# A mixture-of-experts item whose token columns are gathered by GpSimd instead of by transposes and matmuls on TensorE

## The chip, the core and the metric

The program runs on one core of a Trainium2 chip. The metric is the device time of one execution in microseconds (us). Two executions of the same kernel differ by a few tenths of a per cent. TensorE is called PE in the rows, VectorE DVE, ScalarE ACT, GpSimd POOL and SyncE SP; PEld is PE's weight load, and a q behind an engine's name is that engine's sequencer, which loads registers, branches and issues work.

## What is computed

```python
attn = sigmoid(q @ k.T / 8 - log(448)) @ v        # 4 batches, 12 heads, 448 tokens, 64 per head
x = attn as [1792 tokens, 768]
# first layer: tokens with x @ w_skip > 0 go to expert argmax(x @ w_gate)
x[sel] += gate * (relu(x[sel] @ w1[e]) @ w2[e])   # w1[e] 768 x 1024, w2[e] 1024 x 768
# second layer: expert by cosine similarity; its result is the output
out = gate * (relu(x @ v1[e]) @ v2[e])
```

In each layer every token has one of 8 experts. With these inputs, the first layer works on batches 2 and 3 alone: all 448 tokens of batch 2 share an expert, and of batch 3 there are 407 tokens of one expert and 41 of another. In the second layer three batches are of one expert each, and batch 2 has 443 tokens of one and 5 of another.

## The kernel before

Activations lie transposed: `xT` is [128, 6, 1792], with 768 = 6 x 128 features on the partitions and one column for each token. After the attention there are **blocks**, one for a batch and its most frequent expert: block 0 and block 1 of the first layer, then four blocks of the second. `dense` runs a block over eight slices `f` of 128 hidden features. `h(f)` is 18 matmuls (each product is three, since both factors are split in a rounded part and the rest, `mm3`), `y(f-1)` is 18 more that accumulate in six PSUM banks `YS`. Between them stand **sub-steps** 0 to 15: `sub(2f)` behind `h(f)` and `sub(2f+1)` behind `y(f-1)`. Sub-steps 0 and 1 both stand behind `h(0)`, since there is no `y` yet. What is handed to a sub-step is written into every engine's program at that place. The order is written by hand: `schedule` takes a dictionary of steps by sub-step (`at`) and a list of further steps (`prep`) with the sub-steps they go to. Each engine runs its own list in order.

The tokens of a batch that are not of the block's expert are an **item** of up to 64 tokens (`Item`). Item 0 (the 41 tokens) is run beside block 1, item 1 (the 5 tokens) beside the last block. An item needs its tokens as 64 columns `XB` of 6 x 128 features. Before, this is made so:

- `regs` loads batch, expert and position from the list `LI` in SBUF into registers of DVE, ACT and SP. `copy` copies the batch's columns from `xT` to the tile `STG` (three copies on DVE, three on ACT).
- `select` makes on DVE the 0/1 matrices `SEL`, which say which of 4 x 112 tokens goes to which of 64 places, and `GRC`, which holds each token's gate and its row number less 4096.
- Six `turn`s transpose `STG` on PE into token rows `ROW`, with one ACT copy each. `gather` (16 matmuls by `SEL`) picks the 64 rows, `gatherT` (3 transposes) turns them back into columns in a part of `ROW`.
- `gate` makes the gates and, for item 0, the transposed `SEL`.
- `first` and `second` load the expert's two weight matrices in four quarters. `h(0)`, `h(1)` (24 matmuls each) compute two halves of the hidden features, `hT` transposes them (2 transposes and a DVE copy), and behind the block `finish` runs the 32 matmuls of the second product, `y`.

In the profiled lines, item 0 has `regs` and `copy` at sub-step 3, `turn` at 4 to 9, `select` at 7, `gather` at 10, `gatherT` and `gate` at 11, `h(0)` at 12, `hT(0)` at 13, `h(1)` at 14, `hT(1)` at 15. Item 1 has `regs` and `copy` at 1, `turn` at 2 to 7, `select` at 5, `gather` at 8, `gatherT` at 9, `gate` at 10, the rest as item 0. Behind block 1 stands `add_y`, six DVE additions of `YS` to `xT`, and then the item's `y`, which writes `YS[0]`. Behind the last block stand copies of `YS` to `STG` (ACT and DVE in turn), transposes, scaled rows in `ROW`, two stores (one of SP, one of ACT), then the item's `y` and its scattered store, which waits for both.

Two PSUM banks (`bank`) serve `h(f)` and all small steps in turn: whoever takes a bank waits for those who read it last.

Of the kernel before, what the change touches and what calls it, by code (L numbers as in the profile page):

```python
# [12 lines left out]
I32 = mybir.dt.int32  # L13
AF = mybir.ActivationFunctionType
ALU = mybir.AluOpType
# [6 lines left out]
def sigmoid_attention_moe_moe_kernel(  # L22
# [15 lines left out]
    nc = tc.nc  # L38
# [26 lines left out]
    def bank(name):  # L65
        if not BANKS:
            return psA.tile([128, 512], F32, tag="psA", name=name)
        turn[0] ^= 1
        return BANKS[turn[0]]

    def spare():
        turn[1] ^= 1
        return XG[turn[1]]
# [428 lines left out]
    def merge(*steps):  # L502

        out = {}
        for t in steps:
            for k in sorted(t):
                f = t[k]
                out.setdefault(k, []).extend(f if isinstance(f, list) else [f])
        return out

    def schedule(at, prep, slots):

        assert len(slots) == len(prep)
        return merge(at, *({k: f} for k, f in zip(slots, prep)))
# [166 lines left out]
    def batch_cols(p, b):  # L681
        return xT[:, p, :].rearrange("q (b s) -> q b s", s=S)[:, ds(b, 1), :].rearrange("q o s -> q (o s)")
# [74 lines left out]
    ROW = wp.tile([128, C * DM], F32, tag="row", name="row")  # L757
    SELT = wp.tile([128, S], F32R, tag="selT", name="selT")
    SEL = wp.tile([128, 4 * 128], F32, tag="sel", name="sel")
    XB = ROW[:, 3 * DM : 3 * DM + ND * TL].rearrange("p (c t) -> p c t", t=TL)  # L760
    SMALL = wp.tile([128, 16], F32, tag="small", name="small")
    POSC, GS, IDX = SMALL[:P, 0:C], SMALL[:, 12:14], SMALL[:, 14:15].bitcast(I32)
    GRC = SMALL[:P, 4:12].rearrange("p (c t) -> p c t", t=2)
# [105 lines left out]
    class Item:  # L869


        def __init__(self, m, i):
            self.m, self.i = m, i
            self.wa, self.wb, self.R = (w1, w2, R1) if m == 0 else (v1, v2, R2)

        def regs(self):
            L, i, xe = self.R.LI, self.i, [ENG.Activation, ENG.DVE]
# [18 lines left out]
                    self.wb[ds(self.e, 1), u * 256 : (u + 1) * 256, :].rearrange("o (g p) d -> p (o g) d", p=128),  # L896
                )

        def copy(self):
            for d in range(ND):  # L900
                o = STG[:, d * S : (d + 1) * S]
                if d % 2:
                    nc.vector.tensor_copy(o, batch_cols(d, self.b))
                else:
                    nc.scalar.activation(o, batch_cols(d, self.b), AF.Copy)

        def select(self):
            R, j = self.R, self.j
            nc.vector.tensor_single_scalar(
# [15 lines left out]
                self.R.LI[0:1, ds(self.i + NL, 1)], engines=[ENG.DVE], min_val=0, max_val=NE - 1  # L925
            )

        def turn(self, d):


            def f():
                ps = bank("ps_xn")
                for c in range(C):
                    o = d * S + c * P
                    nc.tensor.transpose(ps[:P, c * 128 : (c + 1) * 128], STG[:, o : o + P], ident)
                o = ROW[:P].rearrange("p (c d) -> p c d", c=C)[:, :, d * 128 : (d + 1) * 128]
                nc.scalar.activation(o, ps[:P, :].rearrange("p (c d) -> p c d", c=C), AF.Copy)

            return f

        def gather(self):

            hw = DM // 2
            ps = bank("ps_xg")
            for c in range(C):
                for g in range(2):
                    nc.tensor.matmul(
                        ps[TL * g : TL * g + TL, :hw], lhsT=SEL[:P, c * 128 : c * 128 + TL],
                        rhs=ROW[:P, c * DM + g * hw : c * DM + g * hw + hw], start=c == 0, stop=c == C - 1,
                    )  # L950
            self.xg = spare()
            nc.scalar.activation(self.xg[:, :hw], ps[:, :hw], AF.Copy)

        def gatherT(self):
            ps = bank("ps_xs")
            for i in range(3):
                nc.tensor.transpose(ps[:, i * 128 : i * 128 + 128], self.xg[:, i * 128 : i * 128 + 128], ident)
            nc.scalar.activation(
                XB.rearrange("p (g i) t -> p i g t", g=2), ps[:, :384].rearrange("p (i g t) -> p i g t", i=3, g=2), AF.Copy
            )  # L960

        def gate(self):
            ps = bank("ps_gs")
# [10 lines left out]
        def h(self, s):  # L974


            def f():
                ps = bank("ps_h2")
                for c in range(ND):
                    for g in range(2):  # L980
                        nc.tensor.matmul(
                            ps[TL * g : TL * g + TL, :256], lhsT=XB[:, c, :],
                            rhs=as1(QUART[2 * s + g])[:, c, :], start=c == 0, stop=c == ND - 1,
                        )
                hs = self.hs = spare()
                nc.scalar.activation(hs[:, :256], ps[:, :256], AF.Relu)

            return f
# [37 lines left out]

        def ready(self, k0):

            prep = [self.turn(d) for d in range(ND)] + [self.gather, self.gatherT, self.gate]
            at = merge({k0: [self.regs, self.copy], k0 + 4: self.select}, {5: [lambda: self.first(0)]}, {  # L1030
                7: [lambda: self.first(1)], 9: [lambda: self.first(2)], 11: [lambda: self.first(3)],
                12: [self.h(0)], 13: [self.hT(0), lambda: self.second(0, 1)],
                14: [self.h(1)], 15: [self.hT(1), lambda: self.second(2, 3)],
            })
            return at, prep

        def now(self, hooks=()):

            hooks = list(hooks) + [None] * 3
            self.regs()  # L1040
            self.first(0, 1, 2, 3)
            self.copy()
            self.select()
            for f in self.ready(0)[1]:
                f()
            self.h(0)()
            self.hT(0)()
            self.second(0, 1)
            self.h(1)()
            self.hT(1)()  # L1050
            self.second(2, 3)
            self.finish(hooks)

        def finish(self, hooks):
# [97 lines left out]
    def units1(e):  # L1152
        def f(k):
            u, r = k // 4, k % 4
            if r == 0 and u + 2 < NU:
                load_unit(w1, w2, e, u + 2)
            if u + 1 < NU and r % 2 == 0:
                for g in split_unit(u + 1)[:3] if r == 0 else split_unit(u + 1)[3:]:
                    g()

        return f

    def beside(units, steps):
        steps = merge(steps)

        def sub(k):
            for i in (k - 0.5, k):
                if i == k:
                    units(k)
                for f in steps.get(i, ()):  # L1170
                    f()

        return sub
# [42 lines left out]
    def block1(j):  # L1216

        b, e = rest_regs(j - 1)
        xs = XST[j % 2]

        def r2():
            if j > 1:
                return {}
            f = route2_steps(0, XST[0])
            return at_subs((1, 4, 6, 2, 3, 5, 6, 8), f[:3] + f[6:])

        def general():
            with tc.If(count(R1) > 0) as cmp:
                it = Item(0, 0)
                at, prep = it.ready(3)  # L1230
                dense(xs, beside(units1(e), schedule(merge(r2(), at), prep, (4, 5, 6, 7, 8, 9, 10, 11, 11))))
                add_y(b)
                it.finish(start2(j > 1))
            with cmp.Else():
                dense(xs, beside(units1(e), r2()))
                add_y(b)
                for f in start2(j > 1):
                    f()
                nothing()
            rare()  # L1240

        def last():
            with tc.If(nc.values_load(R1.LI[0:1, 3 * NL + 3 : 3 * NL + 4], min_val=0, max_val=NL) > 0) as cmp:
                it = Item(0, 0)
                at, prep = it.ready(3)
                one, two, three = start2(j > 1)
                steps = schedule(merge({12: one, 14: three}, r2(), at), prep, (4, 5, 6, 7, 8, 9, 10, 11, 11))
                dense(xs, beside(units1(e), steps))
                add_y(b)
                it.finish([two, None, None])  # L1250
            with cmp.Else():
                general()

        if j == B - 1:
            last()
            return
        with tc.If(NB["n"] > j) as cmp:
            dense(xs, beside(units1(e), merge(r2(), next_dense(j))))
            add_y(b)
            block1(j + 1)  # L1260
        with cmp.Else():
            last()
# [113 lines left out]
    for j in range(B):  # L1376
# [36 lines left out]
            continue  # L1413
        with tc.If(count(R2) > 0) as cmp:  # L1414
            it = Item(1, 0)
            at, prep = it.ready(1)
            dense(xs, beside(units2, schedule(merge(todo, at), prep, (2, 3, 4, 5, 6, 7, 8, 9, 10))))
            finish(j, b, True)()
            it.finish([None] * 3)
            info = mybir.DependencyInfo(mybir.DependencyClass.Sync, mybir.DependencyReason.DATA)  # L1420
            tc.add_manual_dep(it.put().ins, STORES[0].ins.name, info, reason="the rows it lands on")
# [40 lines left out]
```

## Time and profile before

| what | us |
|---|---|
| median of 3 runs (lowest, highest) | 590.76 (589.76, 591.95) |
| the profiled execution | 592.26 |
| its span (first to last instruction) | 590.5 |
| PE busy | 573.4 (97%) |
| DVE busy | 304.9 (52%) |
| ACT busy | 276.3 (47%) |
| POOL busy | 7.5 (1%) |

Block 1 with item 0 lies between 220 and 301 us, the last block with item 1 between 497 and 581 us. Matmuls are pipelined, so what a step costs PE is read from start to start in the order of time, not from busy time. The granted clock of PE is 9 tenths or more in every slice of the page behind the first.

### The profile page before, as it was taken

The numbers are of one execution on the slowest core, as the hardware profiler recorded it, in microseconds if no ns is written. First come the engines' busy times: TensorE is split into PE (matmuls) and PEld (weight loads), VectorE is DVE, ScalarE is ACT, GpSimd is POOL, SyncE is SP. The second block draws the span as 40 slices with busy tenths as digits, with TensorE's granted clock in tenths as the row PEclk, the third lists the DMA queues.
The fourth block names the chain that finished last, engine by engine and source line by source line (L and its number), as shares of the span: only waits on it lengthen the run. The fifth ranks groups of instructions, "written<-read, shape, count | busy, mean of one in ns | idle before, by whom it ended". The sixth has DMA issues, their size and how long they took to land. (4 is left out here: it accounts for less than half of the span.)

```text
span 590.5 us, 9926 instructions
## 1 busy us (share of the span) xinstructions
PE 573.4 (97%) x3720; PEld 437.7 (74%) x3720; DVE 304.9 (52%) x770; ACT 276.3 (47%) x451; POOL 7.5 (1%) x15
## 2 busy tenths in 40 slices
PE   7999999999999999999999999999999999999993
PEld 4453644534499988988868999979997999898881
DVE  2443444246857677661359663587357663542131
ACT  3766676667932364541146322932365322543020
POOL 2010000000000000000000000000000000000000
PEclk7999999999999999999999999999999999999998
DMA  9988698975341414235553060713226060742433
GB/s 150 136 126 123 96 134 108 130 102 174 129 157 60 157 41 165 68 108 185 192 199 126 2 213 1 237 71 125 89 84 226 0 215 0 245 156 67 161 108 100
DMA packets 139862, 73.31 MB, mean 124 GB/s; under 512 B 103858, under 2 KB 129798, under 8 KB 139792
## 3 DMA queue, kind: packets, MB, share of 16 engines
q1 hardware_dynamic: 116384, 65.94, 42.0%
q10 hardware_dynamic: 23216, 6.43, 6.4%
q8 instruction: 37, 0.61, 0.5%
q14 instruction: 33, 0.27, 0.1%
q0 software_dynamic: 192, 0.07, 0.1%
HBM read 66.90 MB, written 5.70 MB: 123 GB/s over the span
## 5 line engine op out<-in xcount | busy, mean ns | idle before, releaser
L787 PE MATMUL bank<-xs,h 128*128 128x448 f32 x288 | 107.6, 374 | 1.8 <-DVE hl L808 0.5
L807 ACT ACTIVATE hh<-bank 128x448 fp32r<-128x448 f32 x48 | 26.0, 542 | 176.4 <-PE bank L789 165.8
L787 PE MATMUL y<-hh,h 128*128 128x448 f32 x288 | 108.5, 377 | 0.0
L788 PE MATMUL y<-hl,h 128*128 128x448 f32 x288 | 105.6, 367 | 0.0
L789 PE MATMUL y<-hh,l 128*128 128x448 f32 x288 | 105.6, 367 | 0.0
L788 PE MATMUL bank<-xs,h 128*128 128x448 f32 x288 | 105.5, 366 | 0.0
L789 PE MATMUL bank<-xs,l 128*128 128x448 f32 x288 | 105.2, 365 | 0.1
L607 ACT ACTIVATE A<-psS,bias 128x896 f32<-128x896 f32 x84 | 83.5, 1007 | 36.3 <-PE psS L603 35.9
L603 PE MATMUL psS<-qT,kT 64*64 64x448 f32 x672 | 90.5, 554 | 0.0
L808 DVE SCALAR_TENSOR_TENSOR hl<-bank,hh 128x448 fp32r<-128x448 f32 x48 | 29.9, 623 | 113.5 <-ACT hh L807 111.9
L778 DVE TENSOR_TENSOR l<-r,h 128x512 fp32r<-128x512 f32 (+1 forms) x115 | 85.4, 792 | 4.7 <-ACT h L777 3.0
L621 PE MATMUL psO<-A,v 64*64 64x448 f32 x672 | 87.3, 538 | 0.0
L777 ACT ACTIVATE h<-r 128x512 fp32r<-128x512 f32 (+1 forms) x115 | 74.6, 710 | 0.0
L787 PEld LDWEIGHTS bank<-xs,h 128*128 128x128 f32 x288 | 54.0, 187 | 11.2 <-DVE hl L808 2.9
L787 PEld LDWEIGHTS y<-hh,h 128*128 128x128 f32 x288 | 54.1, 188 | 8.1 <-issue 2.9
L621 PEld LDWEIGHTS psO<-A,v 64*64 64x64 f32 x672 | 34.0, 133 | 33.7 <-issue 22.8
L789 PEld LDWEIGHTS bank<-xs,l 128*128 128x128 f32 x288 | 54.1, 188 | 5.3 <-DVE l L778 0.4
L789 PEld LDWEIGHTS y<-hh,l 128*128 128x128 f32 x288 | 54.1, 188 | 4.9
L603 PEld LDWEIGHTS psS<-qT,kT 64*64 64x64 f32 x672 | 32.2, 135 | 34.2 <-issue 20.0
L788 PEld LDWEIGHTS y<-hl,h 128*128 128x128 f32 x288 | 54.2, 188 | 4.6 <-issue 0.2
L788 PEld LDWEIGHTS bank<-xs,h 128*128 128x128 f32 x288 | 54.1, 188 | 4.2
L529 DVE COPY xT<-psO 64x448 f32<-64x448 f32 x24 | 14.9, 622 | 46.8 <-PE psO L621 46.6
(253 smaller groups left out, 453.5 us busy)
## 6 DMA issues: line engine op xcount, KB each, us to landing
r<-in_moe_w_dram SPq DMA_DIRECT2D x62, 768.0 KB, 6.0
v<-in_v_dram ACTq DMA_DIRECT2D x48, 112.0 KB, 3.6
k<-in_k_dram SPq DMA_DIRECT2D x44, 112.0 KB, 3.5
q<-in_q_dram SPq DMA_DIRECT2D x44, 112.0 KB, 4.2
out_dram<-row SPq DMA_DIRECT2D x3, 1344.0 KB, 6.9
out_dram<-row SPq DMA_DIRECT2D x1, 896.0 KB, 5.5
stg<-in_moe_w_dram SPq DMA_DIRECT2D x1, 768.0 KB, 8.7
row<-in_moe_w_dram SPq DMA_DIRECT2D x1, 768.0 KB, 9.9
```

The lines of the kernel that those rows point to most:

```text
L529: nc.vector.tensor_copy(x, ps[64 * j : 64 * j + 64, :S])
L603: nc.tensor.matmul(ps[KT * i : KT * i + KT, j, :S], lhsT=kT[r, i, h * KT : (h + 1) * KT], rhs=qT[r, i], start=True, stop=True,)
L607: nc.scalar.activation(at, ps[:, :, :S], AF.Sigmoid, bias=bias, scale=1.0 / math.sqrt(D))
L621: nc.tensor.matmul(ST[w, "o"][i][D * j : D * j + D, :S], lhsT=t[r, j, h, :], rhs=at[r, j, :], start=h == 0, stop=h == NH - 1,)
L777: nc.scalar.activation(dst_h, src, AF.Copy)
L778: nc.vector.tensor_sub(dst_l, src, dst_h.bitcast(F32))
L787: nc.tensor.matmul(ps, lhsT=ah, rhs=bh, start=first, stop=False)
L788: nc.tensor.matmul(ps, lhsT=ah, rhs=bl, start=False, stop=False)
L789: nc.tensor.matmul(ps, lhsT=al, rhs=bh, start=False, stop=last)
L807: nc.scalar.activation(a, ps[:, :S], AF.Relu)
L808: nc.vector.scalar_tensor_tensor(l, ps[:, :S], 0.0, a.bitcast(F32), op0=ALU.max, op1=ALU.subtract)
```

## The change

An item's columns are copied from `xT` by GpSimd, one token at a time. `places` makes a list of 64 column numbers: 4 matmuls of `GRC`'s row numbers by `SEL` give one row of 64, and a DVE instruction adds 4096, clips and writes it as integers to one partition of the item's tile (`ROW` for item 0, `STG` for item 1). `gather` then has, for each of the 64, a register load on GpSimd and a copy of 128 x 6 elements from that column of `xT`. `copy`, the six `turn`s, the old `gather` and `gatherT` are gone. `places` takes the bank that was used last (`turn[0] ^= 1` ahead of `bank`).

`regs` and `select` go to sub-step 0, `places` and `gather` to 3, `gate` to 7. `h(0)` goes from 12 to 13, `hT(0)` from 13 to 14, `h(1)` from 14 to 15, and `hT(1)` from 15 to behind the block's last `y`, ahead of `add_y` (item 0) or of the copies of `YS` (item 1). The load `second(0, 1)` goes from 13 to 14, `second(2, 3)` stays at 15, now behind `h(1)`.

```diff
-    XB = ROW[:, 3 * DM : 3 * DM + ND * TL].rearrange("p (c t) -> p c t", t=TL)
...
+            home = (ROW, STG)[m]
+            self.xb = home[:, 3 * DM : 3 * DM + ND * TL].rearrange("p (c t) -> p c t", t=TL)
+            self.places_ = home[0:1, 2 * DM : 2 * DM + TL].bitcast(I32)
...
+        def places(self):
+            turn[0] ^= 1
+            ps = bank("ps_pl")
+            for c in range(C):
+                nc.tensor.matmul(
+                    ps[0:1, :TL], lhsT=GRC[:, c, 1:2], rhs=SEL[:P, c * 128 : c * 128 + TL], start=c == 0, stop=c == C - 1
+                )
+            nc.vector.tensor_scalar(self.places_, ps[0:1, :TL], float(SKIP), float(NT - 1), op0=ALU.add, op1=ALU.min)
+
+        def gather(self, t0, t1):
             def f():
...
+                for t in range(t0, t1):
+                    o = nc.values_load(self.places_[0:1, t : t + 1], engines=[ENG.Pool], min_val=0, max_val=NT - 1,
...
+                    nc.gpsimd.tensor_copy(self.xb[:, :, t : t + 1], xT[:, :, ds(o, 1)])
...
-            prep = [self.turn(d) for d in range(ND)] + [self.gather, self.gatherT, self.gate]
-            at = merge({k0: [self.regs, self.copy], k0 + 4: self.select}, {5: [lambda: self.first(0)]}, {
+            prep = [self.places, self.gather(0, TL), self.gate]
+            at = merge({k0: [self.regs, self.select]}, {5: [lambda: self.first(0)]}, {
                 7: [lambda: self.first(1)], 9: [lambda: self.first(2)], 11: [lambda: self.first(3)],
-                12: [self.h(0)], 13: [self.hT(0), lambda: self.second(0, 1)],
-                14: [self.h(1)], 15: [self.hT(1), lambda: self.second(2, 3)],
+                13: [self.h(0)], 14: [self.hT(0), lambda: self.second(0, 1)],
+                15: [self.h(1), lambda: self.second(2, 3)],
             })
...
-                at, prep = it.ready(3)
+                at, prep = it.ready(0)
                 one, two, three = start2(j > 1)
-                steps = schedule(merge({12: one, 14: three}, r2(), at), prep, (4, 5, 6, 7, 8, 9, 10, 11, 11))
+                steps = schedule(merge({12: one, 14: three}, r2(), at), prep, (3, 3, 7))
                 dense(xs, beside(units1(e), steps))
+                it.hT(1)()
                 add_y(b)
```

The same is done where item 1 runs. Three places show how the engines' lists change. In these rows `hl`, `hh` are the two parts of `h(f)`, `l` and `h` those of a weight slice `r`, `sel` and `small` hold `SEL` and `GRC`, `LI` the list, and ISA is a register operation. A bracket names the engines that a row waits for.

DVE at sub-step 0 of block 1. Before:

```order
L808 SCALAR_TENSOR_TENSOR hl_77<-bank_1703,hh_75 128x448 [waits Activation_49]
L778 TENSOR_TENSOR l_1716<-r_91,h_1715 128x512 [waits DMAHW6_49,Activation_49]
L778 TENSOR_TENSOR l_1716<-r_91,h_1715 128x512 [waits Activation_49] x2
L1092 TENSOR_LOAD pb
L689 ISA
L689 TENSOR_TENSOR xs_93<-xT,xs_93 128x448 [waits Activation_49]
```

Now:

```order
L777 TENSOR_TENSOR l_1716<-r_91,h_1715 128x512 [waits Activation_49] x2
L880 TENSOR_LOAD LI_104
L882 TENSOR_LOAD LI_104
L882 ISA x2
L918 TENSOR_LOAD LI_104
L918 ISA x2
L903 ISA
L903 TENSOR_SCALAR small<-POS_97 112x4
L907 ISA
L907 TENSOR_TENSOR small<-small,kcol 112x4 [waits DVE_49]
L908 ISA
L908 COPY small<-gr_357 112x8
```

Three register loads and `select` (its last rows, four `sel` of L912, follow) now stand between the weight slice and everything behind it: `hl` of `h(1)`, the next slice and the routing step of sub-step 3. At sub-step 3 itself, three loads and copies have gone from DVE, and the list of columns (L930) stands there.

POOL in block 1. Before, behind the branch into the block:

```order
L1243 TENSOR_LOAD LI_104 [waits DVE_49]
L1243 COMPARE_AND_BRANCH
L1243 UNCONDITIONAL_BRANCH [waits Pool_sequencer_49]
L1064 TENSOR_LOAD LI_104
L1228 COMPARE_AND_BRANCH
```

Now:

```order
L1224 TENSOR_LOAD LI_104 [waits DVE_49]
L1224 COMPARE_AND_BRANCH
L937 TENSOR_LOAD row [waits DVE_49,Activation_49]
L939 ISA
L939 COPY row<-xT 128x6 [waits DVE_49,PE_49,DMASW1_49,Activation_49,DMASW2_49,Pool_49]
L937 TENSOR_LOAD row
L939 ISA
L939 COPY row<-xT 128x6
```

POOL had nothing to compute in a block; it now has 64 times a load, a register operation and a copy, and only the first waits for other engines.

DVE at the end of block 1. Before:

```order
L808 SCALAR_TENSOR_TENSOR hl_78<-bank_1704,hh_76 128x448 [waits DVE_49,Activation_49]
L778 TENSOR_TENSOR l_1712<-stg,h_1711 128x512 [waits DMAHW0_49,Activation_49]
L778 TENSOR_TENSOR l_1712<-stg,h_1711 128x512 [waits Activation_49] x2
L995 COPY sel<-bank_1704 128x256 [waits PE_49]
L1178 ISA
L1178 TENSOR_TENSOR xT<-xT,y_1705 128x448 [waits PE_49]
```

Now:

```order
L807 SCALAR_TENSOR_TENSOR hl_78<-bank_1703,hh_76 128x448 [waits DVE_49,Activation_49]
L777 TENSOR_TENSOR l_1712<-stg,h_1711 128x512 [waits DMAHW0_49,Activation_49]
L777 TENSOR_TENSOR l_1712<-stg,h_1711 128x512 [waits Activation_49] x2
L976 COPY sel<-bank_1704 128x256 [waits PE_49] x2
L1158 ISA
L1158 TENSOR_TENSOR xT<-xT,y_1705 128x448 [waits Pool_49]
```

Both copies of `hT` now stand ahead of `add_y`, and the second waits for transposes that PE runs behind the block's last `y`.

## Rows read from the trace of the kernel before

**Rows 1.** The page: busy us (share of the span) and instructions of an engine.

```profile
PE 573.4 (97%) x3720; PEld 437.7 (74%) x3720; DVE 304.9 (52%) x770; ACT 276.3 (47%) x451; POOL 7.5 (1%) x15
```

**Rows 2.** Order of time, PE: start us, duration us, line, operation, out<-in, tile, shape.

```profile
306.52 0.36 PE L787 MATMUL bank<-xs,h 128*128 128x448 f32 x1
310.19 0.37 PE L787 MATMUL y<-hh,h 128*128 128x448 f32 x1
```

**Rows 3.** Order of time, PE: item 0's steps at sub-steps 8 to 12.

```profile
254.73 0.60 PE L935 MATMUL bank<-ident,stg 128*112 128x128 f32 x4
258.82 0.60 PE L935 MATMUL bank<-ident,stg 128*112 128x128 f32 x4
263.01 2.80 PE L947 MATMUL bank<-row,sel 112*64 112x384 f32 x16
...
269.50 0.49 PE L957 MATMUL bank<-ident,xg 128*128 128x128 f32 x3
269.82 0.95 PE L965 MATMUL bank<-small,sel 112*128 112x2 f32 x8
...
274.84 2.81 PE L981 MATMUL bank<-r,row 128*64 128x256 f32 x24
```

**Rows 4.** Order of time, PE: small matmuls of block 0's end, and sub-step 3 of block 1.

```profile
215.32 0.83 PE L454 MATMUL bank<-pm,pc 128*1 128x64 f32 x12
...
233.99 0.46 PE L787 MATMUL bank<-xs,h 128*128 128x448 f32 x1
```

**Rows 5.** Order of time, DVE in block 1: idle before it and its releaser in brackets.

```profile
234.24 0.27 DVE L257 TENSOR_REDUCE lgs<-bank 112x36 f32<-112x108 f32 x1 [1.20 <-PE bank L256]
...
235.51 0.22 DVE L275 TENSOR_TENSOR OH<-d,t 112x32 f32<-112x32 f32 x1
...
255.10 0.17 DVE L909 TENSOR_SCALAR small<-POS 112x4 f32 x1 [0.74 <-issue]
...
255.51 0.87 DVE L918 TENSOR_SCALAR sel<-io,small 112x128 f32<-112x128 f32 x4
```

**Rows 6.** Order of time, DVE and then PE, in the last block.

```profile
510.82 1.00 DVE L903 COPY stg<-xT 128x448 f32 x3 [4.07 <-issue]
511.73 0.62 DVE L808 SCALAR_TENSOR_TENSOR hl<-bank,hh 128x448 fp32r<-128x448 f32 x1
...
512.40 0.65 PE L935 MATMUL bank<-ident,stg 128*112 128x128 f32 x4 [0.85 <-DVE hl L808]
```

**Rows 7.** Sequencers by line: count, duration ns min/median/max, first and last start us.

```profile
L1243 POOLq TENSOR_LOAD <-LI x1: 293/293/293, 217.3 to 217.3; - x1
L1284 POOLq TENSOR_LOAD <-pa x1: 499/499/499, 138.5 to 138.5; - x1
L878 DVEq TENSOR_LOAD <-LI x2: 304/756/1208, 235.5 to 505.9; - x2
L924 DVEq FUSED_REGOPS  x2: 190/190/190, 254.6 to 519.3; - x2
```

**Rows 8.** Order of time, POOL: an instruction on few elements.

```profile
4.80 0.19 POOL L104 IOTA rid_i<- 112x16 int32 x1
```

**Rows 9.** Two stretches, DVE instructions of L778 alone: us, busy (count), PEclk, DMA share, GB/s.

```profile
236.90:274.00 37.10, 7.44 (x10) 1.00 0.36 114
514.80:551.00 36.20, 7.42 (x10) 1.00 0.39 131
```

**Rows 10.** Order of time: ends of block 1 (DVE) and of the last block (ACT, POOL).

```profile
292.24 0.42 DVE L995 COPY sel<-bank 128x256 f32<-128x256 f32 x1 [3.74 <-PE bank L994]
292.85 3.66 DVE L1178 TENSOR_TENSOR xT<-xT,y 128x448 f32 x6 [0.19 <-PE y L789]
...
577.79 0.38 ACTq L1354 DMA_DIRECT2D out_dram<-row  x1
...
585.17 1.08 POOL L1020 DMA_INDIRECT out_dram<-xg,small  x1 [550.23 <-SPq L1427]
```

**Rows 11.** Issues of the line of `second`, all eight: time to landing.

```profile
DMA to landing us min/median/max: 4.4/5.9/7.3
```

More of the change, by code (lines that the diff above doesn't have):

```diff
@@ L897, in second @@
                 )
[L899 to L905, printed above, removed]
         def select(self):
@@ L926, in e_dve @@
             )
-        def turn(self, d):
-            def f():
[L932 to L937, printed above, removed]
-            return f
[L941 to L960, printed above, removed]
+        def places(self):
[7 more added lines that the diff above has]
+        def gather(self, t0, t1):
+            def f():
+                for t in range(t0, t1):
+                    o = nc.values_load(self.places_[0:1, t : t + 1], engines=[ENG.Pool], min_val=0, max_val=NT - 1,
+                                       skip_runtime_bounds_check_because="places() clamps it to 0 .. NT - 1")
+                    nc.gpsimd.tensor_copy(self.xb[:, :, t : t + 1], xT[:, :, ds(o, 1)])
+            return f
         def gate(self):
@@ L981, in f @@
                         nc.tensor.matmul(
-                            ps[TL * g : TL * g + TL, :256], lhsT=XB[:, c, :],
+                            ps[TL * g : TL * g + TL, :256], lhsT=self.xb[:, c, :],
                             rhs=as1(QUART[2 * s + g])[:, c, :], start=c == 0, stop=c == ND - 1,
@@ L1041, in now @@
             self.first(0, 1, 2, 3)
-            self.copy()
             self.select()
@@ L1049, in now @@
             self.h(1)()
+            self.second(2, 3)
             self.hT(1)()
-            self.second(2, 3)
             self.finish(hooks)
@@ L1229, in general @@
                 it = Item(0, 0)
-                at, prep = it.ready(3)
-                dense(xs, beside(units1(e), schedule(merge(r2(), at), prep, (4, 5, 6, 7, 8, 9, 10, 11, 11))))
+                at, prep = it.ready(0)
+                dense(xs, beside(units1(e), schedule(merge(r2(), at), prep, (3, 3, 7))))
+                it.hT(1)()
                 add_y(b)
@@ L1244, in last @@
                 it = Item(0, 0)
-                at, prep = it.ready(3)
+                at, prep = it.ready(0)
                 one, two, three = start2(j > 1)
-                steps = schedule(merge({12: one, 14: three}, r2(), at), prep, (4, 5, 6, 7, 8, 9, 10, 11, 11))
+                steps = schedule(merge({12: one, 14: three}, r2(), at), prep, (3, 3, 7))
                 dense(xs, beside(units1(e), steps))
+                it.hT(1)()
                 add_y(b)
@@ L1415, in sigmoid_attention_moe_moe_kernel @@
             it = Item(1, 0)
-            at, prep = it.ready(1)
-            dense(xs, beside(units2, schedule(merge(todo, at), prep, (2, 3, 4, 5, 6, 7, 8, 9, 10))))
+            at, prep = it.ready(0)
+            dense(xs, beside(units2, schedule(merge(todo, at), prep, (3, 3, 7))))
+            it.hT(1)()
             finish(j, b, True)()
```

## The prediction

> **What bounds the kernel now.** I read the page's busy times first, then the order of time on PE through the two blocks that carry an item, then DVE's list and the sequencers' register loads there. PE is busy 97% of the span and POOL 1% [rows 1]: whatever a block's PE list holds is paid in full, and POOL's time is free until PE waits for it. A half-step of 18 matmuls with nothing beside it takes 310.19 - 306.52 = 3.67 us [rows 2]. What a step costs PE is the distance between two steps less 3.67.
>
> **What goes from PE.** Per item:
> - a `turn`: 258.82 - 254.73 = 4.09, less 3.67 is 0.42; six are 2.5 us [rows 3];
> - the old `gather`: 269.50 - 263.01 = 6.49, less 3.67 is 2.82 [rows 3];
> - `gatherT`: 269.82 - 269.50 = 0.32 [rows 3].
>
> That is 5.66 us, 11.3 for both items, all of it on PE's own path. The six ACT copies behind the turns, three ACT and three DVE copies of the batch go too, off the path; I count nothing for them. `gate`, `h` and `hT` are the same work elsewhere. (`gate` takes 274.84 - 269.82 - 3.67 = 1.35 us [rows 3].)
>
> **What comes to PE.** `places` is 4 matmuls of 64 columns into one row. The nearest are 12 such in 0.83 us busy, pipelined [rows 4], so at most 0.28 for four; I take 0.3 with the change of shape, 0.6 for both items.
>
> **Where the list waits.** `places` needs `select`, which now stands early in DVE's list.
> - Item 0. `select` is 255.51 + 0.87 - 255.10 = 1.28 us [rows 5]; its register loads can run ahead while DVE subtracts weight slices. It pushes back `hl` of `h(1)`, the next slice and the routing reduction L257, which before had been idle 1.20 us ahead of 234.24 [rows 5]. So L257 starts only 0.1 to 0.3 later, at about 234.5. But `places` takes the very bank that L257 reads, so PE, which went on at 233.99 [rows 4], stands until L257 has ended, about 234.8: 0.8 us. Bounds: 0.5 (L257 not moved) and 2.1 (all of `select` in front of it).
> - Item 1. Three register loads on DVE took 4.07 us, since each load took up to 1.2 us or more there against 0.30 elsewhere [rows 6, 7]; three are left (the batch is no longer needed, the expert is loaded now). In place of the copies of 1.00 [rows 6] stands `select`, 1.28 and a check of registers, about 0.2 [rows 7]. `hl` of `h(1)` moves from 511.73 to about 512.3, and PE takes up `places` at 513.0 instead of the turn at 512.40. Since the turn of sub-step 2 is gone, PE comes there 0.4 earlier, so its wait grows from 0.85 [rows 6] to 1.9: 1.05 lost. Bounds: 0.5 and 2.
>
> **The end of the block.** `hT(1)` now stands behind the last `y`, and DVE's second copy of it ahead of the additions. Before, that copy had been done when the first addition started, and the additions ran beside `y(7)` [rows 10]. Now the item's `y`, which writes `YS[0]`, waits on PE for: hand-over 0.1, copy 0.42, hand-over 0.1, first addition 0.61 (3.66 / 6) [rows 10]. That is 1.2 us for item 0. For item 1 the same copy stands ahead of DVE's three copies of `YS`, then come the transposes, the scaled rows and the store that ACT issued at 577.79; POOL's scattered store waits for the stores until 585.17 [rows 10], so a delay of the rows is a delay of the end, while the item's `y` is not late. DVE's chain is put off by 0.4 to 1.7; I take 1.1. The load `second(2, 3)` is issued behind `h(1)`, which now has only `y(7)`, `hT(1)`, the wait and half of the item's `y` in front of its use: 3.7 + 0.3 + 1.2 + 2.7 = 7.9 us against a landing of 5.9, at most 7.3 [rows 11]. I cost it at nothing; without the wait of 1.2 it would be short by up to 0.6.
>
> **Whether POOL is in time.** This decides. POOL starts when the list is written. For item 0, the list follows L257's chain, 1.5 us (234.24 to 235.51 and 0.22 [rows 5]): about 236.2. PE comes to `h(0)` ten half-steps behind `places`: 235.1 + 36.7 + 1.35 for `gate` + 0.35 for a routing step = 273.5. That leaves 37.3 us, **0.58 us for each of 64 columns**. For item 1: list behind `hl` and two weight subtractions (0.74 each [rows 9]; I allow 1.8) at about 514.9; `h(0)` at 513.3 + 36.7 + 0.8 = 550.8, so 35.9 us or **0.56**.
>
> No row shows such a column. The nearest is DVE's `select`, whose first instruction was kept waiting 0.74 us by a load, a register operation of 0.19 and a check, then its own register operation [rows 5, 7]. The new column has the load and one register operation, no check: 0.74 - 0.22 = 0.52. Below, POOL's load alone is 0.29 [rows 7]. Above, if a copy doesn't run beside the next load: 0.52 + 0.19, the price of an instruction on 16 elements [rows 8], is 0.71. I take 0.52, since loads on DVE ran while its datapath worked: 33.3 us, in time by 4.0 and 2.6.
>
> **Sum.** 11.3 - 0.6 - 0.8 - 1.05 - 1.2 - 1.1 = 6.6 us. The profiled execution of 592.26 (span 590.5) becomes 585.7; the median, 1.5 lower, becomes **584.2 us**.
>
> **Rivals.**
> - *The copy and the next load don't overlap*, 0.71 a column: 45.4 us, late by 8.1 and 9.5. PE stands 17.6 us at `h(0)`: 590.8 - 6.6 + 17.6 = **601.8**, slower. It decides from 0.62 a column on, where the two waits have eaten 6.6 us. For it: nothing shows POOL running a load ahead of a copy. Against: what DVE does.
> - *Loads on POOL stay long.* Its first was 499 ns [rows 7]; then a column takes 0.52 + 0.21 = 0.73, 46.7 us, late by 9.4 and 10.8: **604**. Against it: the later one is 293 [rows 7], and the long loads on DVE fall in the store of the rows before [rows 6], over when POOL starts. The Trainium skill, DMA: Bandwidth & Descriptors, section "Latency and other measured facts", gives `tensor_load` a floor of about 600 ns. By that figure a column would take 0.83 and the kernel some 617; the trace's 293 disagrees.
> - *DVE holds POOL off.* If POOL's copies and its list stand still while DVE subtracts one tile of SBUF from another, 7.44 and 7.42 us are added [rows 9]: 40.7 us, late by 3.4 and 4.8: **592.4**. In the trace POOL computes nothing beside a block, so no row is for or against it. A backlog of short copies can be worked off between subtractions, which speaks against the full price. The Trainium skill, GPSIMD Engine Reference, section "Specifications", says that POOL's SBUF interfaces are shared with VectorE, with contention for DVE instructions with two SBUF inputs; no run here shows it.
> - *A little late:* 0.60 a column, 38.4 us, late by 1.1 and 2.5: **587.8**. Or the waits at list and end are at their upper bounds (2.1, 2, 1.7): 587.
>
> **Chances.** In time 0.55 (580.5 to 586.5); a little late or dearer waits 0.17 (586.5 to 590); held off by DVE 0.10; copies not overlapped 0.12; long loads 0.06. The low end is near the sum without any wait at list and end, 590.8 - 10.7 = 580.1. The range 580.5 to 593 leaves out the two slow cases, 0.18. About 0.5% (3 us) is what a measurement can tell from no change: faster than 587.8 has 0.55 and half of 0.17, so 0.63; within it 0.18; slower 0.19.
>
> **What would show it.** In the new profile, loads on POOL of 0.3 and columns every 0.5 us, some 33 us in all, and PE waiting for no POOL copy at `h(0)`; sub-steps 4 to 12 at 3.7 instead of 4.1; a wait of about 0.8 and 1.9 us at `places`; about 1.2 us ahead of item 0's `y`. A wait of PE on POOL at either `h(0)` makes the price of a column the wrong step; PE idle elsewhere makes it the list or the end.

## The result, and the profile after

The changed kernel takes **584.57 us** (median of 4 runs, 583.48 to 584.82); the kernel before, beside it, 590.38. The ratio is 0.9892, with a 95% interval of 0.9877 to 0.9908: 5.8 us or 1.1% faster. 584.2 was forecast.

The page of the changed kernel, to be read against [rows 1]: busy us, share of the span and instructions of each engine.

```profile
PE 563.3 (97%) x3650; PEld 432.0 (74%) x3650; DVE 302.4 (52%) x766; ACT 264.4 (45%) x429; POOL 41.7 (7%) x143
```

PE lost 10.1 us of busy time and is as full as before; POOL went from 7.5 to 41.7. PE in the order of time (start us, duration us, line, operation, out<-in, shape, and in brackets the idle time before it with its releaser): first matmul of block 1, of the block behind it and of the last block, first before, then after.

```profile
220.41 0.45 PE L787 MATMUL bank<-xs,h 128*128 128x448 f32 x1 [0.33 <-DVE xT L1178]
301.55 0.44 PE L787 MATMUL bank<-xs,h 128*128 128x448 f32 x1 [0.39 <-issue]
497.32 0.37 PE L787 MATMUL bank<-xs,h 128*128 128x448 f32 x1
```

```profile
220.08 0.44 PE L786 MATMUL bank<-xs,h 128*128 128x448 f32 x1 [0.57 <-DVE xT L1158]
297.57 0.44 PE L786 MATMUL bank<-xs,h 128*128 128x448 f32 x1 [0.40 <-issue]
493.21 0.37 PE L786 MATMUL bank<-xs,h 128*128 128x448 f32 x1
```

Block 1 shrank from 301.55 - 220.41 = 81.14 to 77.49 us, the last block (to the end of the span) from 93.18 to 88.29. All else is within 0.4. These profiles differ by 9.0 us in span, the medians by 5.8: the profiled execution of before is the highest of its runs, that of after the lowest. Of the last block's 4.9, 2.0 lie behind ACT's last store: 577.79 to 590.5 before [rows 10], 570.81 to 581.5 after. The work left there is the same in both: the item's `y`, the landing of the stores, which the scattered store waits for (585.17 - 577.79 = 7.4 us before, 577.01 - 570.81 = 6.2 after), and POOL's last instructions. One profile of each doesn't tell whether these 2.0 come from the change.

Now the places of which the prediction spoke. PE after the change: the list of item 0 and of item 1, their `h(0)`, item 0's `y`, item 1's last transposes.

```profile
234.22 0.61 PE L927 MATMUL bank<-sel,small 112*1 112x64 f32 x8 [0.36 <-DVE lgs L257]
508.96 0.61 PE L927 MATMUL bank<-sel,small 112*1 112x64 f32 x8 [1.90 <-DVE hl L807]
...
273.41 0.87 PE L962 MATMUL bank<-r,row 128*64 128x256 f32 x6
547.47 1.30 PE L962 MATMUL bank<-r,stg 128*64 128x256 f32 x10
...
291.79 5.38 PE L986 MATMUL y<-r,sel 128*64 128x384 f32 x32 [1.04 <-DVE xT L1158]
565.42 0.40 PE L1321 MATMUL bank<-ident,stg 128*112 128x128 f32 x2 [0.61 <-DVE sel L976]
```

Four waits stand where they were forecast, and none at `h(0)`. POOL by line (count, ns min/median/max, first and last start us):

```profile
L937 POOLq TENSOR_LOAD <-row x64: 284/286/298, 235.6 to 266.1; - x64
L937 POOLq TENSOR_LOAD <-stg x64: 283/285/319, 510.8 to 540.7; - x64
L939 POOLq FUSED_REGOPS  x128: 37/37/54, 235.9 to 541.0; - x128
L939 POOL COPY row<-xT x64: 188/194/931, 236.3 to 266.5; 128x6 f32 x64
L939 POOL COPY stg<-xT x64: 190/195/935, 511.4 to 541.1; 128x6 f32 x64
```

A list of 64 columns takes 30 us, so POOL is done 6.7 us (273.41 - 266.7) and 6.1 us (547.47 - 541.3) before PE needs the columns. The forecast was 4.0 and 2.6.

### The profile page after: what moved, and what is told of

It is laid out like the page before. It is cut to its first block, busy times and chain, and to the rows that moved or that the text cites. A ratio compares the mean times of both kernels' runs of the same rounds, so it can differ in the third digit from the quotient of the medians.

```text
span 581.5 us, 10119 instructions
## 1 busy us (share of the span) xinstructions
PE 563.3 (97%) x3650; PEld 432.0 (74%) x3650; DVE 302.4 (52%) x766; ACT 264.4 (45%) x429; POOL 41.7 (7%) x143
## 5 line engine op out<-in xcount | busy, mean ns | idle before, releaser
L529 DVE COPY xT<-psO 64x448 f32<-64x448 f32 x24 | 14.9, 621 | 46.1 <-PE psO L621 45.9
```

Of the source, the lines that this page charges most:

```text
L529: nc.vector.tensor_copy(x, ps[64 * j : 64 * j + 64, :S])
```

## Experiments

Ten kernels. "Block 1" and "last block" are the stretches above, each of one profiled execution, so they tell where a difference lies and the medians how large it is. The kernel before was measured beside each group: 590.38 with after, 591.15 with e1 to e4, 590.79 with e5 to e8, 591.25 with e9 and e10. So a difference to after that is taken from two medians is uncertain by up to 0.9 us, and the ratios are the better measure: by them e1 lies 2.1 us below after, e6 5.0, and e9 3.3 above it.

| kernel | median us | ratio to before (95%) | block 1 | last block |
|---|---|---|---|---|
| before | 590.4 to 591.3 | | 81.14 | 93.18 |
| after | 584.57 | 0.9892 (0.9877 to 0.9908) | 77.49 | 88.29 |
| e1 `hT` in the block | 581.70 | 0.9856 (0.9835 to 0.9878) | 76.46 | 88.59 |
| e2 list at 4 | 583.77 | 0.9886 (0.9868 to 0.9904) | 78.90 | 87.46 |
| e3 four columns | 583.27 | 0.9879 (0.9860 to 0.9898) | 77.83 | 87.63 |
| e4 before without turns | 581.71 | 0.9856 (0.9836 to 0.9876) | 75.48 | 83.74 |
| e5 loads ahead | 582.48 | 0.9859 (0.9835 to 0.9883) | 78.10 | 86.44 |
| e6 e1 and e5 | **579.06** | 0.9807 (0.9785 to 0.9828) | 76.15 | 85.12 |
| e7 two copies, one place | 618.13 | 1.0457 (1.0429 to 1.0485) | 93.82 | 106.60 |
| e8 two loads | 584.77 | 0.9906 (0.9873 to 0.9939) | 77.86 | 88.77 |
| e9 two copies, two places | 588.13 | 0.9948 (0.9932 to 0.9965) | 79.12 | 92.50 |
| e10 e9 in e6 | 594.29 | 1.0043 (1.0024 to 1.0063) | 83.80 | 93.81 |

### The removed work by itself (e4)

```diff
-            prep = [self.turn(d) for d in range(ND)] + [self.gather, self.gatherT, self.gate]
+            prep = [lambda: None] * 8 + [self.gate]
```

> The kernel before with the six turns, the gather and the transposes behind it left out for both items (the batch is still copied, the selection and the gate stay), so nothing fetches the item's tokens. This measures the removed PE work by itself. Theory (all of it lay on PE's path, 5.66 us for each item): 590.4 - 11.3 = 579.1. Rival (a part of it lay beside waits of PE that stay, for DVE or a weight load): 581 to 584, with PE idle where the turns stood.

Block 1 fell by 81.14 - 75.48 = 5.66 us, the forecast; that it agrees to the hundredth is chance, that it agrees is not: the distance of two steps less a bare half-step is what a step costs on PE. The last block fell by more than 5.66, since the wait of 0.85 at the first turn [rows 6] went too and the stretch behind PE's last matmul took 6.9 us instead of the 9.5 of before's profile. Yet the median is 2.6 above the theory (1.9, if the theory is counted from the 591.15 beside it). The order of time on PE in e4, at the start of the block behind block 1, and then stretches (us, busy and count of PE, PEld, DVE, ACT, POOL, granted clock, DMA share, GB/s):

```profile
294.59 0.44 PE L787 MATMUL bank<-xs,h 128*128 128x448 f32 x1 [0.47 <-issue]
299.60 0.70 PE L787 MATMUL bank<-xs,h 128*128 128x448 f32 x1 [2.94 <-issue]
```

```profile
296.00:300.00 4.00, 1.06 (x5) 0.67 (x4) 2.49 (x4) 1.00 (x2) 0.00 (x0) 0.96 0.84 293
300.00:303.00 3.00, 3.00 (x9) 2.65 (x9) 0.00 (x0) 0.00 (x0) 0.00 (x0) 0.50 1.08 383
```

PE stands 2.94 us with no releaser in the profile, and behind that its clock is at the lower level (1.2 GHz) for 3 us. This block, the one behind block 1, takes 362.67 - 294.59 = 68.1 us here and 63.4 in before, after and every other kernel, 4.7 more. So the removal was worth what was forecast where the work had stood, and this kernel gave back a part elsewhere. Within the stop the trace has a packet of 16 KB of the instruction queue q8, on its way from 297.33 to 298.27; that PE waited for instructions is likely, and not shown.

### Is POOL's time free? (e3, e8, e9, e10, e7)

e3 gathers 4 columns of 64 (`self.gather(0, 4)`).

> The changed kernel with 4 of the 64 columns gathered for each item (the other 60 are left out, so the items compute with what lies there). Theory (POOL's 30 us for each item lie wholly beside PE's work): 584.6, within 0.5. Rival (POOL's copies hold DVE or the memory up, and PE pays for that somewhere in the block): 583 or below.

583.27, between the two expectations: runs from 581.7 to 584.1, those of after from 583.5 to 584.8, and the intervals of the ratios overlap. Block 1 is no shorter (77.83), the last block by 0.7, all of it behind PE's last matmul (7.0 us instead of 7.7). Nor do POOL's copies hold DVE up: DVE's 115 subtractions of weight slices took 793 ns on average after the change and 792 before. POOL's other 28 us cost next to nothing, at most the 1.3 between the medians.

e8 writes the line of the load twice.

> The changed kernel with every place loaded twice by POOL ahead of its one copy. Theory (the load and its register operation set the pitch, and time of POOL is free until PE has to wait): 0.47 + 0.29 + 0.04 = 0.80, 51.2 us, late by 14.1 and 15.1: 584.6 + 29.2 = 613.8, all of it as PE waiting for POOL at the two h(0). Rival (something else than the load sets the pitch): 0.47 to 0.6, 584.6.

The edit didn't do what it says. Lines of POOL in e8, then its first columns in the order of time:

```profile
L937 POOLq EVENT_SEMAPHORE  x128: 17/17/18207, 216.3 to 545.2; - x128
L939 POOLq TENSOR_LOAD <-row x64: 283/284/300, 234.5 to 270.0; - x64
```

```profile
235.87 0.20 POOL L941 COPY row<-xT 128x6 f32 x1 [0.36 <-issue]
236.43 0.20 POOL L941 COPY row<-xT 128x6 f32 x1 [0.36 <-issue]
```

The first load, of which nothing is made, became a semaphore instruction of 17 ns, and a column went from 0.47 to 0.55 us. So neither theory on the load was tested. But POOL worked 5 us longer for each item and was still in time, at 584.77 (583.07 to 586.48): inside its room its time is free, as far as a spread of 3.4 us can tell. The row of PE at both `h(0)` shows no wait for POOL.

e7 copies each column twice.

```diff
+                    nc.gpsimd.tensor_copy(self.xb[:, :, t : t + 1], xT[:, :, ds(o, 1)])
```

> The changed kernel with every column copied twice to the same place by POOL, one load for both. Theory (POOL's load of the next place runs beside the copy, so the sequencer sets the pitch of 0.47 us): the pitch grows by the issue of one copy at most, to under 0.55; 64 x 0.55 = 35.2 us is in time (30.4 + 6.7 and 30.0 + 6.1), so 584.6. Rival (load and copy don't overlap, 0.47 = 0.28 + 0.19): 0.66, 42.2 us, late by 5.1 and 6.1: 595.8, with PE waiting for POOL at h(0).

Both were wrong on the price: 0.72 us for a column. POOL in the order of time, and PE at `h(0)` of both items:

```profile
236.72 0.20 POOL L940 COPY row<-xT 128x6 f32 x1
237.18 0.20 POOL L939 COPY row<-xT 128x6 f32 x1 [0.26 <-issue]
237.44 0.19 POOL L940 COPY row<-xT 128x6 f32 x1
237.90 0.19 POOL L939 COPY row<-xT 128x6 f32 x1 [0.27 <-issue]
...
287.21 3.32 PE L963 MATMUL bank<-r,row 128*64 128x256 f32 x14 [13.64 <-POOL row L940]
577.27 3.32 PE L963 MATMUL bank<-r,stg 128*64 128x256 f32 x14 [13.53 <-POOL stg L940]
```

The second copy writes where the first one wrote, so it waits for its end on a semaphore, and POOL's sequencer waits with it and can't start the next load (the first copy ends at 236.66, the load starts at 236.71). That is an order that I had added, not the price of a copy. e9 sends the second copy to a free place (`self.free`, behind the list in the item's tile).

> The changed kernel with a second copy of every column by POOL, to a free place, so that it waits for nothing (the second copy of the run with two copies to one place waited for the first one's end, and a column cost 0.72 us there). Theory (POOL's load runs beside the copies, and a further copy costs the sequencer its register operation and its issue, 0.12 us): 0.58 to 0.59 a column, 64 x 0.12 = 7.5 us more in each item, against room of 6.7 and 6.1: late by 0.8 and 1.4, 584.6 + 2.2 = 586.8. Rival (DVE's subtractions hold the copies off, and with two copies a column the backlog is not worked off: in the run before 50.4 us for 64 columns at 0.72, 4.3 us more than 46.1): late by 5.1 and 5.7, 595 or more.

POOL and PE in e9:

```profile
235.80 0.20 POOL L940 COPY row<-xT 128x6 f32 x1 [202.11 <-PE bank L788]
235.93 0.19 POOL L941 COPY row<-xT 128x6 f32 x1
236.38 0.20 POOL L940 COPY row<-xT 128x6 f32 x1 [0.26 <-issue]
...
273.77 2.88 PE L964 MATMUL bank<-r,row 128*64 128x256 f32 x24 [0.69 <-POOL row L940]
```

A column costs 0.58, as the theory says: copies start 0.13 apart and stand under the load of 0.286. The end is late by 0.69 for item 0 (0.8 expected) and at most 0.3 for item 1. 64 columns took 38.0 us where 0.58 x 64 is 37.1; the 0.9 are three stops of POOL's sequencer of 0.3 to 0.4 us each, not DVE's hold (more on them in the part on why the prediction held), so the rival's 4.3 falls. The time is 588.13, 1.3 above the expectation, and not because PE waits for columns: behind item 1's list the clock fell (0.75 in the stretch from 509 to 513 us, a half-step of 5.32 instead of 3.78, 1.5 us), and the last block ended 2.7 us later behind its last step, where POOL's closing semaphore came 2.3 us after the instruction ahead of it. e10 has it too, and e7 is as late: behind PE's last matmul the three kernels with 128 copies more in POOL's list take 10.0 to 10.4 us, the other changed kernels 7.0 to 8.1. In e9 and e10 a packet of 8 KB of the instruction queue q14 lands 1.2 us ahead of the end of that stop (583.75 and 584.99 in e9). So it is likely that POOL waits there for a part of its longer list; no run tests it.

> The same second copy in the kernel with h at sub-steps 12 to 15 and the register loads ahead of the block (579.1), where POOL's last column is ready 3.1 and 3.5 us ahead of h(0). Theory (time of POOL beyond the room is paid one for one): late by 7.5 - 3.1 = 4.4 and 4.0, 579.1 + 8.4 = 587.5, with PE waiting for POOL at both h(0). Rival (the granted clock also falls behind such a wait, as behind the waits of 13.6 us, where a wait was followed by some 2.1 us more): up to 591.

PE in e10, and the stretches around the first of its waits (columns as in e4):

```profile
273.56 5.46 PE L966 MATMUL bank<-r,row 128*64 128x256 f32 x24 [4.49 <-POOL row L942]
551.86 4.57 PE L966 MATMUL bank<-r,stg 128*64 128x256 f32 x24 [4.42 <-POOL stg L942]
```

```profile
269.00:274.00 5.00, 0.51 (x3) 0.37 (x4) 0.62 (x1) 0.54 (x1) 2.58 (x16) 0.86 0.85 307
274.00:279.00 5.00, 5.00 (x25) 3.14 (x21) 0.00 (x0) 0.00 (x0) 0.00 (x0) 0.50 0.02 6
```

The waits are those of the theory (4.4 and 4.0 expected), the time is not: 594.29 against 587.5, above the rival's 591 too. Each `h(0)` with its half-step grew by 7.2 and 6.2 us against e6, with PE at half its clock for 5 us and more behind the first wait, and at 0.58 on average for the first 4.1 us behind the second; the rest is the 2.4 us at the end. So lateness isn't paid one for one.

### The waits at the list (e2, e5)

e2 puts list and columns at sub-step 4 (`prep` at 4, 4, 7).

> The changed kernel with the list and POOL's columns one sub-step later, at 4; h and hT stay. Theory (PE's wait at the list comes from DVE's late select): the waits of 0.36 and 1.90 us at the list are gone, since DVE has 3.7 us more, and POOL, that ends up to 3.7 us later, is still ahead of h(0): 584.6 - 2.3 = 582.3. Rival (DVE is behind there anyway, and the wait only moves to the next instruction that needs DVE): 584.6. Rival (POOL late for item 1): above 584.6 with a wait on POOL at h(0).

Wrong: 583.77. PE at the two lists in e2:

```profile
238.34 0.61 PE L927 MATMUL bank<-sel,small 112*1 112x64 f32 x8 [1.35 <-DVE hl L807]
512.83 0.61 PE L927 MATMUL bank<-sel,small 112*1 112x64 f32 x8 [1.35 <-DVE hl L807]
```

The same wait, 1.35, in both. `places` turns the two banks once, so it takes the bank that was used last. Behind a `y` (odd sub-steps) its readers have had a half-step; behind an `h(f)` (even ones) it holds that `h`, and `places` waits for ACT's ReLU and DVE's `hl` of it. So at sub-step 4 the list waits for DVE even where DVE isn't behind: block 1 lost 1.4, the last block won 0.8.

e5 leaves the list at 3 and moves item 1's register loads ahead of the last block's `dense`:

```diff
             it = Item(1, 0)
+            it.regs()
+            it.ed = it.e_dve()
             at, prep = it.ready(0)
```

> The changed kernel with item 1's register loads (batch, count, expert) ahead of the last block, where DVE is idle for 3.1 us, and not behind the stores of its rows, where three of them kept DVE 4.47 us. Theory (PE's wait of 1.90 us at item 1's list is made by these loads): DVE's second hl of the block is done some 4 us earlier, the wait is gone, POOL keeps its 6.1 us of room: 584.6 - 1.9 = 582.7. Rival (the loads are as long there, or DVE is behind for another reason): 584.6 with the wait still there.

582.48, and the wait is gone. The loads of DVE by line, after and then e5 (one of each pair is item 1's, the last start tells when), and from the order of time PE at item 1's list in e5:

```profile
L880 DVEq TENSOR_LOAD <-LI x2: 317/754/1190, 226.2 to 501.8; - x2
L918 DVEq TENSOR_LOAD <-LI x2: 301/1050/1798, 227.4 to 504.7; - x2
```

```profile
L880 DVEq TENSOR_LOAD <-LI x2: 312/314/316, 226.2 to 495.6; - x2
L920 DVEq TENSOR_LOAD <-LI x2: 301/303/305, 227.4 to 496.7; - x2
```

```profile
507.65 0.61 PE L929 MATMUL bank<-sel,small 112*1 112x64 f32 x8
```

A load that took 1.2 to 1.8 us at 502 to 506 takes 0.3 six to eight microseconds earlier, in a hole of DVE, and the wait of 1.9 us comes back in full.

### The end of the block (e1, e6)

e1 puts `h` and `hT` back to 12 to 15 and leaves out `hT(1)` behind the block.

```diff
-                13: [self.h(0)], 14: [self.hT(0), lambda: self.second(0, 1)],
-                15: [self.h(1), lambda: self.second(2, 3)],
+                12: [self.h(0)], 13: [self.hT(0), lambda: self.second(0, 1)],
+                14: [self.h(1)], 15: [self.hT(1), lambda: self.second(2, 3)],
...
-                it.hT(1)()
```

> The changed kernel with h(0), hT(0), h(1), hT(1) back at sub-steps 12 to 15, as before the change, and no hT(1) behind the last y; the list stays at 3 and POOL's columns stay. Theory (the end of the block costs a wait, and POOL has more room than it needs): the 1.04 us ahead of item 0's y and the 0.61 us ahead of item 1's last transposes go, POOL is still done 3.0 and 2.4 us ahead of h(0) (6.7 and 6.1 less a half-step of 3.67): 584.6 - 1.0 - 0.4 to 1.1 = 582.5 to 583.2. Rival (the waits at the end cover something else that is as late, as the second weights or the stores): 584.6, no change. Rival (POOL stops PE one sub-step earlier): a wait on POOL at h(0), 586 or more.

581.70, 2.9 less than after and 0.8 below the expectation, and PE waits for POOL nowhere: the later `h(0)` bought room that wasn't needed and cost a wait at both ends. Block 1 won 1.0. In the last block the gain is hidden: PE stood 1.88 us at the list as it did after the change, but here the clock fell behind it. Stretches of e1, then of after (columns as in e4):

```profile
509.00:511.00 2.00, 2.00 (x7) 1.79 (x6) 0.00 (x0) 0.00 (x0) 0.78 (x4) 0.50 1.09 364
```

```profile
509.00:511.00 2.00, 2.00 (x15) 1.79 (x16) 1.76 (x3) 0.00 (x0) 0.00 (x0) 1.00 1.04 393
```

The same step took 5.32 us instead of 3.78. The profile is not alone in it: the granted clock of e1's four runs is 0.988 to 0.991, that of after's 0.995 or 0.996 in three and 0.987 in one. e6 is e1 with the loads of e5, so that this wait doesn't arise.

> The run before last's two edits together: h and hT at sub-steps 12 to 15 as in the kernel before, and item 1's register loads ahead of the last block. In the first of these alone PE had stood 1.88 us at item 1's list, and the granted clock then was 0.50 to 0.78 from 507 to 511 us, 1.54 us dearer. Theory (without the wait there is no drop of the clock behind it): 581.7 - 1.9 - 1.5 = 578.3. Rival (the wait stays or comes back at the next step that needs DVE): 581.7.

579.06 (578.19 to 580.33): 5.5 us below the changed kernel by the medians, 1.9% below before, the fastest version here. Its clock is at 1.00 through both item blocks, no wait of PE over 0.4 us is left in them, and POOL is ready 3.0 and 3.4 us early. The last block of e6 is 1.3 us shorter than that of e5, which is the price of the end of the block for item 1.

## Why the prediction held

- **Removed work, 11.3 us**: 5.66 for item 0 shown by e4.
- **POOL in time**, the step that decided: right, and the reason is right. I took 0.52 us for a column; it is 0.47. The size has some luck in it: the 0.52 held a register operation of 0.19, from DVE, which takes 0.037 on POOL; load and register operation make 0.32, and the rest of the 0.47 is time between instructions. In one stretch of the changed kernel loads and copies stand like this:

```profile
L937 POOLq TENSOR_LOAD <-row x6: 284/288/293, 236.3 to 238.7; - x6
L939 POOL COPY row<-xT x6: 195/196/197, 236.3 to 238.7; 128x6 f32 x6
```

  The load of the next place starts with the copy of this one, so the copy is covered; the rival without overlap falls, and e9 shows it again (a further copy costs 0.11, not 0.19).
- **Long loads** fall: 283 to 319 ns for 128 loads on POOL. The floor of about 600 ns that the Trainium skill gives for `tensor_load` (DMA: Bandwidth & Descriptors, "Latency and other measured facts") doesn't hold for these loads from SBUF; DVE's, of up to 1.8 us, lie above it.
- **DVE holds POOL off**: single copies grow, the list doesn't. The changed kernel's POOL and then DVE at the same time:

```profile
239.63 0.19 POOL L939 COPY row<-xT 128x6 f32 x1 [0.27 <-issue]
240.48 3.02 POOL L939 COPY row<-xT 128x6 f32 x7 [0.66 <-issue]
```

```profile
239.90 1.89 DVE L777 TENSOR_TENSOR l<-r,h 128x512 fp32r<-128x512 f32 x3
241.70 1.15 DVE L689 TENSOR_TENSOR xs<-xT,xs 128x448 fp32r<-128x448 f32 x2
```

  While DVE subtracts two tiles of SBUF, a copy takes up to 0.93 us instead of 0.19, as the Trainium skill says of DVE's instructions with two SBUF inputs (GPSIMD Engine Reference, "Specifications"). But the sequencer goes on loading, and the backlog is worked off. Over 64 columns the loss is 30.4 - 63 x 0.467 - 0.2 = 0.8 us, not 7.4, and most of it isn't DVE's: 0.39 us stand ahead of the copy at 240.48, between the 9th and the 10th load, and 0.29 between the 51st and the 52nd, at 260 us, where DVE has nothing to do. In e2, whose list starts 5.8 us later, POOL and then DVE show the first of these stops at the same column, with no subtraction beside it:

```profile
245.43 0.19 POOL L939 COPY row<-xT 128x6 f32 x1 [0.27 <-issue]
246.29 0.19 POOL L939 COPY row<-xT 128x6 f32 x1 [0.66 <-issue]
```

```profile
245.47 0.17 DVE L311 SCALAR_TENSOR_TENSOR CE<-PRIM,CNT 128x8 f32<-128x8 f32 x1
247.65 0.62 DVE L807 SCALAR_TENSOR_TENSOR hl<-bank,hh 128x448 fp32r<-128x448 f32 x1 [2.00 <-ACT hh L806]
```

  The stops lie 42 columns of 3 instructions apart, in e9 25 or 26 columns of 5, so always 125 to 130 instructions of POOL; in after and e2 a packet of 8 KB starts on the instruction queue q14 some 0.7 to 1.1 us behind the end of each. They belong to the place in POOL's list, probably to the loading of its instructions, which no run tests; DVE's share of the 0.8 is some 0.1 us. Where the sequencer has to wait for the end of a copy, as in e7, the hold does cost: 50.7 us for item 0's 64 columns where 64 x 0.72 is 46.1, of which these stops make less than 1.
- **The lists**: item 1's wait was forecast as 1.9 and is 1.90. For item 0 it is 0.36 instead of 0.8, but the matmuls cost 234.75 - 234.22 = 0.53 instead of 0.3.
- **The end**: 1.04 for 1.2, and 1.3 for 1.1 (e6 against e5). These two rows and item 1's list were the dear part of the change, and e6 shows that the change could have been had without them.
- **The sum**: 6.6 forecast; 5.8 by the medians. Block 1 gave 3.65 for 5.66 - 0.3 - 0.8 - 1.2 = 3.4. Of the last block's 4.9, without the 2 us behind the last store, 2.9 answer to 5.66 - 0.3 - 1.05 - 1.1 = 3.2. That is 6.5 in one pair of profiles; the 0.7 to the medians are not assigned. A term that I didn't have is the clock: where it falls behind a wait of 1.9 us, 1.5 us are added. In the profile of after it doesn't fall behind the list.

The point of decision, 0.58 us a column for item 0, is confirmed to within a microsecond: e9 has 0.58, and PE waits 0.69 us.

## What to carry to other kernels

Work that is taken off a full engine is worth its distance from start to start, and the engine that takes it over costs nothing as long as it ends in time: count its room, and spend what is left of it on taking steps back out of the places where others wait (e6). Look where register loads stand in an engine's list: the same three loads cost 0.9 us (e5, at 495 to 497 us) or 4.2 us (after, at 502 to 506.5 us). The DMA engines were busy for a share of 0.04 there and 0.98 here; but POOL's loads from 510.8 us on stayed at 0.28 to 0.32 beside a share of 1.06, so a busy DMA alone isn't the cause, and what it is stays open. And a step that borrows one of two banks in turn belongs behind the work that hasn't just written that bank.

## What the hardware showed beyond that

- The register loads of the list from SBUF take 0.28 to 0.32 us on POOL and run beside POOL's copies, but a semaphore wait between two copies stops the loads too (0.72 instead of 0.58 us a column).
- A wait of PE can cost more than its length. Behind 4.4 us of waiting the granted clock was at 0.50 (1.2 GHz for 2.4), once for 5 us and more, and the step cost 6.2 to 7.2. Behind a wait at item 1's list it fell in e1 (1.88 us) and e9 (1.65) and not in after (1.90), e3 (1.95) and e8 (1.93), in one profile of each. What tells these apart no run here shows.
- An engine can stop where the profile names no releaser: 2.94 us on PE in e4, 2.3 us on POOL at the end of e9 and e10, 0.3 to 0.4 us in POOL's list every 125 to 130 instructions. A packet of an instruction queue lies in or near all but one of those looked at here (after, e2, e4, e9, e10); that the packets are the cause is not tested.
